# Every second low part of the summed mixing weights from ScalarE and an adding transfer instead of VectorE

## The chip, the core and the metric

The kernel runs on one core of a Trainium2 chip. The metric is the device time of one execution in microseconds (us); lower is better. A core has five engines that work side by side and each take their instructions in a fixed order: TensorE (PE in the profile; PEld is its loading of stationary operands), VectorE (DVE), ScalarE (ACT), GpSimd (POOL) and SyncE (SP, which here only starts transfers). Transfers are started from SP, ACT and POOL and are carried out by 16 shared DMA engines.

## The reference

The layer has an attention branch and a gated branch over the same normalised input; the change is in the gated branch (`B`).

```python
def _B_ref(x, w_in, w_sp, b_sp, w_out):
    z = _gelu(jnp.einsum("bsd,df->bsf", x, w_in))
    z1 = z[..., :Fh]
    z2 = _layernorm(z[..., Fh:], axis=-1)
    g = jnp.einsum("ts,bsf->btf", w_sp, z2) + b_sp[None, :, None]
    return jnp.einsum("bsf,fd->bsd", z1 * g, w_out)

xn = _layernorm(x, axis=-1)
s = _A_ref(xn, A_wqkv, A_wo)       # 32 heads, 8 taps at distance 2
g = _silu(_B_ref(xn, B_w_in, B_w_sp, B_b_sp, B_w_out))
return x + s * g
```

There are 2048 rows (`S`), 512 features (`D`) and 896 hidden features (`Fh`). `w_sp` is the 2048 x 2048 mixing matrix. All inputs are float32.

## The kernel before

**Two parts for each operand.** TensorE multiplies in a rounded 32-bit form (`F32R`). To keep float32 accuracy, each operand is held as a high part (the value rounded) and a low part (what the rounding left), and each product is three matmuls: high by high, high by low, low by high. `split` (L194) makes the parts: ScalarE copies the raw block into the high tile, which rounds it, and VectorE then writes raw minus high into the low tile. `prep` (L175) fetches a raw block of 128 x 512 (256 KB) by a transfer from SP, takes the next of eight pairs of weight tiles (`whi0..7`, `wlo0..7`; a pair is free again when TensorE has used it for the last time) and calls `split`. The raw blocks go round in four buffers (tag `raw`, `RAW = 4`); one is free again when both of its readers are done.

**The stages.** In order: products for q, k and v (`qkv`, to about 100 us of the profile), the hidden products (`z1`, `z2`, to about 325 us), the mixing product (the `g` matmuls of L823, 325 to 570 us), the output of the gated branch (`b`, L1065 to L1067, to about 650 us) and that of the attention (`s`, the same lines, to the end).

**The mixing product.** It is done for two halves `a` of the columns by a scheme of seven block products, in which some weights are plain blocks of `w_sp` (`plain`, tiles `wsp_`) and some are sums and differences of blocks (`summed`, tiles `ws_`). Those sums were written to the scratch tensor `sums_d` earlier. `block_product` takes eight weight blocks `s` in four pairs. For a pair it runs three matmuls for each of three feature blocks (`ODD`) and each of the two weights, and in some products for a fourth (`odd`). Four products use summed weights, for each half: m6, m7, m5 and m3, so there are 64 such blocks. They stand on TensorE in the order m6a, m6b, m7 (two halves), then m4 with plain weights, m5a, m5b, m3a, m3b.

**What fills the other engines.** The attention is worked on by VectorE during the whole of this time, at a low priority. Its units (`sub`, `h`) have two steps of four rows each: `scores` (tile `pr`), `heads` (tile `lg`), `weighted` (tile `pv`), and in `finish` the folds and a transpose (tile `tt`). The first fold of `pv` (L631) is on POOL, which also starts the loads of `k`, `q` and `v` and the store of `tt` to `o_d`. POOL further stores gates to `g_d` (L914).

**What sets the order.** A scheduler builds each engine's order ahead of time from priorities and its own estimates of times; `pin` keeps some instructions in the order of the program. On the chip each engine only follows its list and waits on semaphores.

Of the kernel before, what the change touches and what calls it, by code (L numbers as in the profile page):

```python
# [11 lines left out]
F32 = mybir.dt.float32  # L12
F32R = mybir.dt.float32r
AF = mybir.ActivationFunctionType
ALU = mybir.AluOpType
# [11 lines left out]
CT = 512  # L27
# [30 lines left out]
def kernel(  # L58
# [13 lines left out]
    nc = tc.nc  # L72
    pins = [True]
    lows, highs, sums_of = [], [], []

    def pin(ins):
        return tc.keep_in_program_order(ins) if pins[0] else ins
# [22 lines left out]
    sums_d = dram.tile([2, 2, HT, P, 2, CT], F32, name="sums_d")  # L100
# [59 lines left out]
    def weight_pair(name):  # L160
        i = next(slot)
        return (
            wts.tile([P, 512], F32R, tag=f"whi{i}", name=name + "h"),
            wts.tile([P, 512], F32R, tag=f"wlo{i}", name=name + "l"),
        )

    def fetch(src, n, name):
        raw = raws.tile([P, 512], F32, tag="raw", name=name + "r", bufs=RAW)
        pin(nc.sync.dma_start(raw[:, :n], src))
        return raw  # L170
# [4 lines left out]
    def prep(src, n, name, raw=None, pair_=None):  # L175
        if raw is None:
            raw = fetch(src, n, name)
        hi, lo = pair_ or weight_pair(name)
        split(hi[:, :n], lo[:, :n], raw[:, :n])
        return hi, lo  # L180

    @contextmanager
# [11 lines left out]
    def split(hi, lo, src):  # L194
        first_ = pin(nc.scalar.activation(hi, src, AF.Copy))  # L195
        highs.append(first_)
        lows.append(pin(nc.vector.tensor_tensor(lo, src, hi.bitcast(F32), op=ALU.subtract)))  # L197
        return first_
# [225 lines left out]
    def weights(g, raw=[None] * KB):  # L424
        return [prep(wqkv[:, g, k, :], GC, f"wqkv_{g}_{k}", raw=raw[k]) for k in range(KB)]
# [69 lines left out]
    for k in range(KB):  # L495
        hi, lo = [planes[:, FB - KB + k, :JC, a] for a in range(2)]
# [196 lines left out]
    for f in range(FB):  # L693
        pair_ = side_pair("w1_last") if f == FB - 1 else None
        wh, wl = prep(w_in1[:, f, :], KB * P, f"w1_{f}", pair_=pair_)
        for c in range(NC):
            pz = mm(f"z1_{f}_{c}")
            for k in range(KB):
                cc = slice(k * P, (k + 1) * P)
                xh, xl = [planes[:, FB - KB + k, c * JC : (c + 1) * JC, a] for a in range(2)]  # L700
                nc.tensor.matmul(pz, wh[:, cc], xh, start=k == 0, stop=False)
                nc.tensor.matmul(pz, wh[:, cc], xl, start=False, stop=False)
                nc.tensor.matmul(pz, wl[:, cc], xh, start=False, stop=k == KB - 1)
            if c % 2 == 0:
                zp = t4(f"z1t_{f}_{c}")
            zt = zp[:, c % 2]
            nc.scalar.activation(zt, pz, AF.Gelu_apprx_tanh)  # L707
            if c % 2:
                nc.scalar.dma_start(z1_d[f, c - 1 : c + 1].rearrange("c p t -> p c t"), zp)
        if f == 2:  # L710
            first_sums(*z1_sums[FB])
        if f < FB - 1:
            first_sums(*z1_sums[f + 1])

    HALF = (slice(0, 512), slice(512, FH))
    WID = (512, FH - 512)
    w2 = {
        (k, h): prep(w_in2[:, k, HALF[h]], WID[h], f"w2_{k}_{h}")
        for h in range(2)
        for k in range(KB)  # L720
# [115 lines left out]
    for n in range(8):  # L836
        a, f = n // 2 % 2, n // 4 * 2 + n % 2
# [30 lines left out]
        return w  # L868

    def summed(a, half_, i):  # L870
        return lambda s: prep(sums_d[a, half_, s, :, i], CT, f"ws_{a}{half_}{i}_{s}")

    def operand(i, s0):
        f0, r0 = ((ODD + 1, 0), (0, 0), (0, HT))[i]
# [122 lines left out]
    def kept(a):  # L997
# [19 lines left out]
    stored_gates(1, 2)  # L1017
    block_product(
        0, "m6a", at(0, LAST), summed(0, 0, 0),
        steps=([T4[0]], [T4[1], seeds], [T4[2]], [T4[3]]),  # L1020
    )
    spill(0)
    block_product(1, "m6b", at(0, LAST), summed(1, 0, 0))
    spill(1)
    vs3 = triple("x3")
    for a in range(2):
        block_product(
            a, "m7", at(0, 0), summed(a, 0, 1), odd(0),
            steps=([T1[2 * a]], [], [T1[2 * a + 1]], []),
        )  # L1030
        for f in range(ODD):
            evict(a, f, vs3[a][f])
# [144 lines left out]
```

## Time and profile before

| what | value |
|---|---|
| median of 3 runs | 696.28 us (693.53 to 700.32) |
| span of the profiled execution | 694.8 us |
| its own time | the page gives its span; the three runs lie between 1.3 us below and 5.5 us above it |
| TensorE, VectorE, ScalarE, POOL busy | 99%, 90%, 40%, 31% of the span |
| granted TensorE clock | 0.999 of full speed |
| summed-weight products on TensorE | 385.2 to 461.6 us (m6, m7), 504.9 to 570.4 us (m5, m3) |

A row of a timeline gives the start (us), the duration (us), the engine, the line, the operation, the output and inputs, and in brackets how long the engine had been idle before and what ended it. A row that groups instructions gives their number, the busy time, the mean in ns, and the idle time before them with what released it. In the rows of stretches stand, after the stretch and its length, the busy times of PE, PEld, DVE, ACT and POOL with the numbers of instructions, the granted clock, the mean share of the DMA engines and GB/s.

### The profile page before, as it was taken

To read this page: it belongs to the slowest core of one execution; us is meant where nothing else is said; L and a number is where in the kernel's file an instruction comes from. 1 tells how busy PE (TensorE), PEld (TensorE's weight loads), DVE (VectorE), ACT (ScalarE), POOL (GpSimd) and SP (SyncE) were. 2 spreads that over 40 slices of the span, in tenths; PEclk is the share of its full clock that TensorE was granted. 3 is DMA by queue.
4 is the path that set the end of the run, shared out by engine and by line. 5 is a ranking of instruction groups with operands and counts; after the bars stand their busy time and mean duration, and the time that the engine had idled before them with its cause. 6 is when DMAs were issued, how large, how long until landed. Compare 5 with 4: busy or idle time off the path is not lost.

```text
span 694.8 us, 9233 instructions
## 1 busy us (share of the span) xinstructions
PE 688.0 (99%) x3084; PEld 572.9 (82%) x3084; DVE 624.9 (90%) x866; ACT 276.2 (40%) x458; POOL 213.3 (31%) x242
## 2 busy tenths in 40 slices
PE   8999999999999999999999999999999999999998
PEld 7888888888888899977888888888888887888886
DVE  6777877999999989899999998999998999999875
ACT  4343333314424256765533544342433444211432
POOL 3105737282343321223123222214021111452320
PEclk9999999999999999999999999999999999999999
DMA  8869899959999865266798878667576683645797
GB/s 269 253 191 303 273 361 374 334 200 352 406 410 363 320 227 189 96 212 221 260 401 281 289 222 305 203 224 264 158 255 215 221 306 118 242 155 167 253 339 267
DMA packets 102223, 182.36 MB, mean 262 GB/s; under 512 B 9184, under 2 KB 45280, under 8 KB 102176
## 3 DMA queue, kind: packets, MB, share of 16 engines
q1 hardware_dynamic: 56624, 102.21, 43.7%
q0 software_dynamic: 13824, 52.24, 20.8%
q10 hardware_dynamic: 31728, 27.33, 11.6%
q8 instruction: 24, 0.39, 0.2%
q14 instruction: 23, 0.19, 0.1%
HBM read 122.42 MB, written 59.32 MB: 262 GB/s over the span
## 4 chain that ended last, share of the span: by engine, by line
PE 68%; DVE 15%; DMA 8%; issue 4%; ACT 3%; POOL 1%; DVEq 0%; ACTq 0%; POOLq 0%; SPq 0%
PE g L823 35%; PE qkv L385 4%; PE qkv L387 4%; PE qkv L386 4%; PE b L1066 4%; PE b L1065 4%; PE b L1067 4%; DMA sb<-in_w_sp 3%; DVE lg L580 2%; DVE pr L573 2%; PE s L1066 2%; PE s L1067 2%; PE s L1065 2%; DMA sums_d<-sb 2%; PE qkv L308 2%
## 5 line engine op out<-in xcount | busy, mean ns | idle before, releaser
L631 POOL TENSOR_TENSOR pv<-pv 128x1024 f32<-128x1024 f32 x29 | 69.6, 2400 | 97.1 <-DVE pv L620 85.1
L573 DVE TENSOR_TENSOR pr<-k,q 128x2048 f32<-128x2048 f32 x32 | 73.6, 2300 | 4.3 <-DMA k<-qkv_d 4.1
L620 DVE TENSOR_TENSOR pv<-v,lg 128x2048 f32<-128x2048 f32 x32 | 74.6, 2331 | 0.9 <-DMA v<-qkv_d 0.4
L580 DVE TENSOR_REDUCE lg<-pr 128x128 f32<-128x2048 f32 x32 | 73.0, 2280 | 0.1
L645 POOL DMA_DIRECT2D o_d<-tt x32 | 18.0, 562 | 141.4 <-DVE tt L644 140.9
L433 ACT ACTIVATE stage<-qkv 128x512 f32<-128x512 f32 x40 | 23.0, 590 | 29.7 <-DMA qkv_d<-stage 19.7
L805 POOL DMA_DIRECT2D ol<-o_d x32 | 17.7, 555 | 36.8 <-DVE BIG L197 11.0
L707 ACT ACTIVATE z1t<-z 128x512 f32<-128x512 f32 x28 | 15.5, 596 | 28.9 <-DMA z_d<-z1t 13.5
L728 PE MATMUL z<-w_0h,BIG 128*128 128x512 f32 x64 | 25.0, 391 | 0.8 <-ACT zt L731 0.8
L1076 ACT ACTIVATE bt<-b 128x512 f32<-128x512 f32 x16 | 9.3, 594 | 39.8 <-PE b L1067 39.8
L730 PE MATMUL z<-w_0h,BIG 128*128 128x512 f32 x64 | 25.0, 391 | 0.0
L729 PE MATMUL z<-w_0l,BIG 128*128 128x512 f32 x64 | 25.0, 391 | 0.0
L752 ACT ACTIVATE zt<-zt,nmz,mvz 128x896 f32<-128x896 f32 x16 | 17.5, 1131 | 18.5 <-POOL nmz L746 18.5
L740 DVE BATCH_NORM_STATS2 zst<-zt 128x6 f32<-128x448 f32 x32 | 19.3, 613 | 6.1 <-ACT zt L731 6.0
L280 DVE TENSOR_TENSOR xT<-xT,mr 128x512 f32<-128x512 f32 x20 | 13.8, 688 | 11.8 <-DMA mr<-mv_d 6.8
L636 DVE TENSOR_TENSOR pv<-pv 128x512 f32<-128x512 f32 x32 | 22.9, 716 | 0.0
L731 ACT ACTIVATE zt<-z 128x512 f32<-128x512 f32 (+1 forms) x32 | 15.9, 536 | 14.2 <-DMA sums_d<-sa 12.8
L730 PE MATMUL z<-w_1h,BIG 128*128 128x384 f32 x64 | 21.5, 336 | 0.0
L728 PE MATMUL z<-w_1h,BIG 128*128 128x384 f32 x64 | 21.5, 335 | 0.0
L729 PE MATMUL z<-w_1l,BIG 128*128 128x384 f32 x64 | 21.4, 335 | 0.0
L195 ACT ACTIVATE BIG<-zl 128x512 fp32r<-128x512 f32 x20 | 12.4, 629 | 22.4 <-DVE zl L893 20.6
L393 POOL TENSOR_TENSOR sb<-sa,sb 128x512 f32<-128x512 f32 x12 | 18.7, 1560 | 5.3 <-DMA sb<-in_w_sp 5.0
(478 smaller groups left out, 2303.6 us busy)
## 6 DMA issues: line engine op xcount, KB each, us to landing
qkv_d<-stage ACTq DMA_DIRECT2D x24, 512.0 KB
v<-qkv_d POOLq DMA_DIRECT2D x14, 704.0 KB, 5.3
k<-qkv_d POOLq DMA_DIRECT2D x13, 704.0 KB, 6.4
sums_d<-sa POOLq DMA_DIRECT2D x14, 512.0 KB, 7.5
sums_d<-sb POOLq DMA_DIRECT2D x14, 512.0 KB, 7.8
z_d<-z1t ACTq DMA_DIRECT2D x14, 512.0 KB
zl<-z_d SPq DMA_DIRECT2D x12, 512.0 KB
tr<-t_d SPq DMA_DIRECT2D x12, 384.0 KB
```

The costliest lines, as they stand in the source:

```text
L385: nc.tensor.matmul(pq, xh[:, k], wh, start=k == 0, stop=False)
L573: line(nc.vector.tensor_tensor(pr, taps(ks[u], j0), qb.unsqueeze(1).to_broadcast([P, W, NJ * CS]), op=ALU.mult))
L580: line(nc.vector.tensor_reduce(lgs[u][:, :, j0 * HS : (j0 + NJ) * HS], pr.rearrange("p w (i d) -> p w i d", d=DH), axis=AX.X, op=ALU.add,))
L620: line(nc.vector.tensor_tensor(pv.rearrange("p w (i d) -> p w i d", d=DH), taps(vs[u], j0).rearrange("p w (i d) -> p w i d", d=DH), lgs[u] ...
L631: eng.tensor_tensor(pv[:, 0:4], pv[:, 0:4], pv[:, 4:8], op=ALU.add)
L728: nc.tensor.matmul(pz, xh[:, k], wh, start=k == 0, stop=False)
L729: nc.tensor.matmul(pz, xh[:, k], wl, start=False, stop=False)
L730: nc.tensor.matmul(pz, xl[:, k], wh, start=False, stop=k == KB - 1)
L823: nc.tensor.matmul(pg, z[a], w[b], start=start and i == 0, stop=stop and i == 2, skip_group_check=seeded)
L1065: nc.tensor.matmul(pp[:, cols], hi, wh, start=k == 0, stop=False)
L1066: nc.tensor.matmul(pp[:, cols], hi, wl, start=False, stop=False)
L1067: nc.tensor.matmul(pp[:, cols], lo, wh, start=False, stop=k == n - 1)
```

## The change

For blocks with an odd `s` (32 of the 64) the low part is made in another way. ScalarE writes the high part as before. ScalarE then writes minus the rounded block into the low tile, and a transfer started from POOL adds the float32 block from `sums_d` to the low tile in place. The result is again raw minus rounded. It is written as float32 by the transfer. VectorE has no part in it. The ScalarE instruction for the low tile is entered in `highs`, behind which the `seeds` are placed. Blocks with an even `s` are made as before.

```diff
+    def prep_added(src, name):
+        raw = fetch(src, CT, name)
+        hi, lo = weight_pair(name)
+        nc.scalar.activation(hi, raw, AF.Copy)
+        highs.append(nc.scalar.activation(lo, raw, AF.Copy, scale=-1.0))
+        nc.gpsimd.dma_start(lo.bitcast(F32), src, accum_op=ALU.add)
+        return hi, lo
+
     def summed(a, half_, i):
-        return lambda s: prep(sums_d[a, half_, s, :, i], CT, f"ws_{a}{half_}{i}_{s}")
+        return lambda s: (prep_added if s % 2 else lambda src, name: prep(src, CT, name))(
+            sums_d[a, half_, s, :, i], f"ws_{a}{half_}{i}_{s}"
+        )
```

The numbers of lines below the new function move by 8 (by 10 behind `summed`). The scheduler places the work anew. On POOL, at the first product with summed weights (m6a, and the start of m6b), the list before reads as follows, beginning at the store of an attention step; `pv` is the fold of a step, `g_d` the store of gates.

```order
L645 DMA o_d<-tt_4_1542 128x256
L631 TENSOR_TENSOR pv_0_1551<-pv_0_1551 128x1024
L914 DMA g_d<-zl_0_3829 128x2x512
L914 DMA g_d<-zl_2_3836 128x2x512
L645 DMA o_d<-tt_0_1571 128x256
L631 TENSOR_TENSOR pv_4_1574<-pv_4_1574 128x1024
L562 DMA v_0_1586<-qkv_d 128x1408
```

With the change the list at the same place is this; the transfers of L187 are the new ones.

```order
L653 DMA o_d<-tt_4_1542 128x256
L187 DMA ws_3l<-sums_d 128x512
L639 TENSOR_TENSOR pv_0_1551<-pv_0_1551 128x1024
L187 DMA ws_5l<-sums_d 128x512
L924 DMA g_d<-zl_0_3829 128x2x512
L924 DMA g_d<-zl_2_3836 128x2x512
L187 DMA ws_7l<-sums_d 128x512
L187 DMA ws_1l<-sums_d 128x512
L653 DMA o_d<-tt_0_1571 128x256
L187 DMA ws_3l<-sums_d 128x512
L639 TENSOR_TENSOR pv_4_1574<-pv_4_1574 128x1024
L570 DMA v_0_1586<-qkv_d 128x1408
```

The new transfers stand between the attention's instructions: that for `ws_3` of m6a behind a store of `tt`, that for `ws_5` behind a fold, and the next row after these is that for `ws_5` of m6b, behind a fold and the load of `v`. That for `ws_1` of m6a stands earlier, behind the load `v_1_1545`.

On VectorE, at the same place, the list before was this (`zl` are gates times banks, `BIG<-tr` low parts of combined `z2` blocks, `sm` and `lg` steps of the softmax).

```order
L197 TENSOR_TENSOR ws_2l<-ws_2r,ws_2h 128x512
L644 STREAM_TRANSPOSE tt_4_1542<-pv_4_1533 128x256
L612 TENSOR_REDUCE sm_1547<-lg_1485 128x32
L197 TENSOR_TENSOR ws_3l<-ws_3r,ws_3h 128x512
L613 RECIPROCAL sm_1547<-sm_1547 128x32
L893 TENSOR_TENSOR zl_0_3829<-g_0_3191,zl_0_3829 128x512
L614 TENSOR_TENSOR lg_1485<-lg_1485,sm_1547 128x256
L197 TENSOR_TENSOR BIG<-tr_2_3907,BIG 128x2x3x128
L197 TENSOR_TENSOR ws_4l<-ws_4r,ws_4h 128x512
L620 TENSOR_TENSOR pv_0_1551<-v_1_1545,lg_1485 128x2048
L580 TENSOR_REDUCE lg_1525<-pr_4_1538 128x8x16
```

Now it is this.

```order
L205 TENSOR_TENSOR ws_2l<-ws_2r,ws_2h 128x512
L652 STREAM_TRANSPOSE tt_4_1542<-pv_4_1533 128x256
L620 TENSOR_REDUCE sm_1547<-lg_1485 128x32
L621 RECIPROCAL sm_1547<-sm_1547 128x32
L622 TENSOR_TENSOR lg_1485<-lg_1485,sm_1547 128x256
L628 TENSOR_TENSOR pv_0_1551<-v_1_1545,lg_1485 128x2048
L588 TENSOR_REDUCE lg_1525<-pr_4_1538 128x8x16
L903 TENSOR_TENSOR zl_0_3829<-g_0_3191,zl_0_3829 128x512
L205 TENSOR_TENSOR BIG<-tr_2_3909,BIG 128x2x3x128
L205 TENSOR_TENSOR ws_4l<-ws_4r,ws_4h 128x512
L903 TENSOR_TENSOR zl_0_3829<-g_1_3192,zl_0_3829 128x512
```

`ws_3l` is gone, and the attention's `pv` now stands ahead of one gate, one low part of `tr` and `ws_4l`.

At the end of the mixing product, where the weights `wout` begin, VectorE's list before was

```order
L197 TENSOR_TENSOR ws_7l<-ws_7r,ws_7h 128x512
L893 TENSOR_TENSOR zl_4_5159<-yl_0_5161,zl_4_5159 128x512
L197 TENSOR_TENSOR wout_0l<-wout_0r,wout_0h 128x512
L893 TENSOR_TENSOR zl_6_5171<-yl_2_5173,zl_6_5171 128x512
L644 STREAM_TRANSPOSE tt_4_1745<-pv_4_1736 128x256
```

and is now

```order
L205 TENSOR_TENSOR ws_6l<-ws_6r,ws_6h 128x512
L581 TENSOR_TENSOR pr_4_1781<-k_0_1764,q_0_1765 128x2048
L205 TENSOR_TENSOR wout_0l<-wout_0r,wout_0h 128x512
L903 TENSOR_TENSOR zl_4_5187<-yl_0_5189,zl_4_5187 128x512
L644 TENSOR_TENSOR pv_4_1776<-pv_4_1776 128x512
```

The fold that follows `wout_0l` there is of the step `pv_4_1776`, two steps of the attention behind that of `pv_4_1736`: at that place VectorE has been given two steps more of attention.

## The prediction

> **What bounds the kernel now.** I read the page's busy shares first, then the busy time by stretches, then what TensorE waited for, and last the timelines of the engines around one product. From the page:
>
> ```profile
> span 694.8 us, 9233 instructions
> PE 688.0 (99%) x3084; PEld 572.9 (82%) x3084; DVE 624.9 (90%) x866; ACT 276.2 (40%) x458; POOL 213.3 (31%) x242
> ```
>
> TensorE is busy for 688.0 of 694.8 us. VectorE, which the change relieves, has 90%. The two stretches in which summed weights are made and used look like this:
>
> ```profile
> 376.00:456.00 80.00, 80.00 (x355) 66.24 (x354) 75.94 (x102) 34.97 (x58) 18.14 (x19) 1.00 0.78 265
> 490.00:570.00 80.00, 80.00 (x355) 66.24 (x354) 77.22 (x111) 30.07 (x52) 12.61 (x13) 1.00 0.69 230
> ```
>
> In both, TensorE runs 355 matmuls in 80 us, one each 0.225 us, with no gap. VectorE is almost full too (75.94 and 77.22), but what it is late with is not what TensorE waits for. All that TensorE waited for is six waits, of which the page of waits gives for the mixing product only the last three below:
>
> ```profile
> PE z L728 <- ACT zt L731: 0.8, 1, 0.8
> ...
> PE g L823 <- ACT g L841: 0.4, 1, 0.4
> PE g L823 <- DVE wsp_1l L197: 0.3, 1, 0.3
> PE g L823 <- ACT BIG L195: 0.2, 1, 0.2
> ```
>
> So TensorE's stream is the bound from end to end, and 0.9 us at most could be won in the mixing product. The rest of VectorE's work can only cost time, by being late, never save any.
>
> **The change part by part: what leaves and what comes.**
>
> ```profile
> L197 DVE TENSOR_TENSOR ws_1l<-ws_1r,ws_1h 128x512 fp32r<-128x512 f32 x8 | 5.4, 678 | 0.0
> L195 ACT ACTIVATE ws_1h<-ws_1r 128x512 fp32r<-128x512 f32 x8 | 5.1, 632 | 5.0 <-DMA ws_1r<-sums_d 4.9
> ```
>
> VectorE loses 32 subtractions of 0.678 us, 21.7 us. By its new list it gets back two steps of attention in the same time, so it stays full. ScalarE gains 32 copies of the form of `ws_1h`, 32 x 0.632 = 20.2 us, some 10 us in each stretch, where it was busy 34.97 and 30.07 of 80: covered by its own idle time. Neither is on TensorE's path, so I count 0 for both. If ScalarE's cover were gone, each low part would come 0.63 us later, and that term is in the sum below anyway, since the copy stands ahead of the transfer.
>
> POOL gains 32 starts of transfers. The DMA engines gain 32 x 256 KB = 8.4 MB in about 160 us, 52 GB/s beside 265 and 230, and the destination is read as well. They are busy 0.78 and 0.69, so there is room, but transfers will take somewhat longer.
>
> What can cost is the new chain of an odd low part: fetched raw block, high copy, low copy, POOL's turn, transfer. Before, it was raw block, high copy, VectorE's turn, 0.68 us.
>
> **The price of the adding transfer.** No transfer of this kind is in the trace. The nearest rows are transfers on POOL's queue in these stretches (KB, us from issue to landing), and plain fetches of the same 256 KB, read as the time from SP's issue to the ScalarE copy that waits for it:
>
> ```profile
> g_d<-zl POOLq DMA_DIRECT2D x3, 512.0 KB, 5.2
> o_d<-tt POOLq DMA_DIRECT2D x12, 128.0 KB, 5.1
> q<-qkv_d POOLq DMA_DIRECT2D x6, 256.0 KB, 6.5
> ```
>
> ```profile
> 380.50 0.32 SPq L169 DMA_DIRECT2D ws_5r<-sums_d  x1
> 394.11 0.32 SPq L169 DMA_DIRECT2D ws_1r<-sums_d  x1
> ```
>
> ```profile
> 387.37 0.64 ACT L195 ACTIVATE ws_5h<-ws_5r 128x512 fp32r<-128x512 f32 x1 [0.64 <-DMA ws_5r<-sums_d]
> 398.18 0.64 ACT L195 ACTIVATE ws_1h<-ws_1r 128x512 fp32r<-128x512 f32 x1 [2.36 <-DMA ws_1r<-sums_d]
> ```
>
> The fetches took 6.9 and 4.1 us. The lower end of the price is 4.1 (as fast as the faster plain fetch). The upper end is 13, twice `q`, if reading the destination and adding doubles a transfer. I take 6.5, the row of `q`: the same size on the same queue, behind another transfer as most of the new ones will be.
>
> A page would have it otherwise: the Trainium skill, "DMA: Bandwidth & Descriptors", in "Anatomy of one DMA — SWDGE (gpsimd) path", fits a transfer from this queue as 2.0 us plus its bytes over 436 GB/s, an estimate of 2.6 us here; the rows above do not bear it out in this loaded kernel (5.1 us for 128 KB), and by it the sum below would be 0.
>
> **The first product, transfer by transfer.** POOL's timeline before at m6a and the start of m6b:
>
> ```profile
> 384.47 0.55 POOL L645 DMA_DIRECT2D o_d<-tt  x1 [3.72 <-DVE tt L644]
> 390.25 2.40 POOL L631 TENSOR_TENSOR pv<-pv 128x1024 f32<-128x1024 f32 x1 [5.22 <-DVE pv L620]
> 395.14 0.73 POOL L914 DMA_DIRECT2D g_d<-zl  x1 [1.09 <-DVE zl L893]
> 407.38 0.58 POOL L645 DMA_DIRECT2D o_d<-tt  x1 [11.51 <-DVE tt L644]
> 413.45 0.57 POOL L562 DMA_DIRECT2D v<-qkv_d  x1
> ```
>
> POOL mostly waits for VectorE's attention, up to 11.51 us at one instruction, and the new transfers now stand in line behind those waits. VectorE's timeline there:
>
> ```profile
> 384.61 0.68 DVE L197 TENSOR_TENSOR ws_3l<-ws_3r,ws_3h 128x512 fp32r<-128x512 f32 x1
> 385.20 0.35 DVE L613 RECIPROCAL sm<-sm 128x32 f32<-128x32 f32 x1
> 385.45 0.64 DVE L893 TENSOR_TENSOR zl<-g,zl 128x512 f32<-128x512 f32 x1
> 386.00 0.42 DVE L614 TENSOR_TENSOR lg<-lg,sm 128x256 f32<-128x256 f32 x1
> 386.33 0.96 DVE L197 TENSOR_TENSOR BIG<-tr,BIG 128x768 fp32r<-128x768 f32 x1
> 387.19 0.70 DVE L197 TENSOR_TENSOR ws_4l<-ws_4r,ws_4h 128x512 fp32r<-128x512 f32 x1
> 387.80 2.30 DVE L620 TENSOR_TENSOR pv<-v,lg 128x2048 f32<-128x2048 f32 x1
> ```
>
> From start to start, `ws_3l` takes 0.59, the gate 0.55, `BIG<-tr` 0.86, `ws_4l` 0.61. All four no longer stand ahead of `pv`, which so starts 2.6 us earlier, at 385.2, and the fold on POOL at 387.65 (it follows by 2.45). TensorE's first uses of the low parts are the deadlines:
>
> ```profile
> 386.13 0.39 PE L823 MATMUL g<-ws_1l,BIG 128*128 128x512 f32 x1
> 390.21 0.39 PE L823 MATMUL g<-ws_3l,BIG 128*128 128x512 f32 x1
> 394.75 0.39 PE L823 MATMUL g<-ws_5l,BIG 128*128 128x512 f32 x1
> 398.37 0.39 PE L823 MATMUL g<-ws_7l,BIG 128*128 128x512 f32 x1
> 406.53 0.39 PE L823 MATMUL g<-ws_3l,BIG 128*128 128x512 f32 x1
> 410.61 0.39 PE L823 MATMUL g<-ws_5l,BIG 128*128 128x512 f32 x1
> ```
>
> With 6.5 us from start to landing, and each delay moving all later deadlines:
>
> - `ws_1` of m6a follows its two copies and starts near 379; it lands at 385.5, in time.
> - `ws_3` stands behind the store of `tt` (384.47 + 0.55), starts at 385.0, lands at 391.5: 1.3 late.
> - `ws_5` stands behind the fold (387.65 + 2.40), starts at 390.05, lands at 396.55 against 394.75 + 1.3: 0.5 late, 1.8 in all.
> - `ws_7` stands behind both stores of gates. VectorE's four gates end about 0.4 us earlier than before, so the second store runs from 394.0 to 394.75 and the transfer lands at 401.25 against 398.37 + 1.8: 1.1 late, 2.9 in all.
> - In m6b, `ws_3` follows the store of the next step. With VectorE's new order I count that store at 402.45 rather than 407.38 (five subtractions and two late gates fewer ahead of it); start 403.0, landing 409.5 against 406.53 + 2.9: 0.1 late. `ws_5` follows a fold and the load of `v`: start 407.2, landing 413.7 against 410.61 + 3.0: 0.1 late. In all 3.1.
>
> Whatever the price, the sum here is about the price less 3.4. Once TensorE has been late by that, the later products find their transfers ahead of it: m7 uses each pair for longer (a fourth feature block).
>
> **The later products.** The tightest is the last weight of m3b:
>
> ```profile
> 557.09 0.68 DVE L197 TENSOR_TENSOR ws_2l<-ws_2r,ws_2h 128x512 fp32r<-128x512 f32 x1
> 558.39 0.42 SPq L169 DMA_DIRECT2D ws_7r<-sums_d  x1
> 564.02 0.64 ACT L195 ACTIVATE ws_7h<-ws_7r 128x512 fp32r<-128x512 f32 x1
> 567.01 0.39 PE L823 MATMUL g<-ws_7l,BIG 128*128 128x512 f32 x1
> ```
>
> Its fetch goes out in SP's order once VectorE has read raw `ws_2`. Copies from 564.02 end at 565.3; a transfer then lands at 571.8 against 567.01 + 3.1: 1.7 late if VectorE comes to `ws_2l` as late as before, 0 if it comes 2 us earlier, as its list (16 subtractions out, one step of attention in up to m5) may let it. I take 0.9.
>
> Sum: 0 + 0 + 3.1 + 0.9 = 4.0 us on a span of 694.8, 698.8. The profile gives no time of its own beyond the span; the median of the three runs is 696.28, 1.5 above the span, so I forecast 700.3 as a median.
>
> **The rivals.**
>
> *The transfers are hidden.* With 4.1 us all six are in time but the last of m6a (0.5) and one of m6b (0.1); m3b is met. That gives 0.6, 696.9. For it: the faster fetch. Against it: every row of POOL's queue is above 5. The rule of the Trainium skill's page "DMA: Bandwidth & Descriptors" named above would give this case, at 696.3.
>
> *The adding transfer is slow and TensorE is fed at its pace (slower).* With 13 us the first product costs 13 - 3.4 = 9.6. A pair of tiles is used for 4.1 us in a period of 16.3 (m6a's `ws_3l` to m6b's is 406.53 - 390.21 = 16.3), which leaves 12.2 us from its release to its next use. Two copies, a start and 13 us are 14.8: 2.6 late in each of m5b, m3a and m3b, 7.8 more. Sum 17.4, 713.7. It decides by over 1% (7 us) from a price of 10.4 us. For it: the destination is read too, the DMA engines are at 0.78, and POOL's line adds waits. Against it: 512 KB on that queue took 5.2.
>
> *VectorE's relief shortens the kernel.* It would have to take away waits of TensorE, and there are 0.9 us of them in this product: 695.4 at best. That the change only shifts VectorE's work is certain from its new list.
>
> **How the numbers follow.** Chances: my forecast of a small loss (697 to 703) 0.48, hidden 0.20, slow transfer 0.29, relief 0.03. About 1% (7 us) is what a measurement of this kernel can tell from no change. The first two lie within 1%, the third above it; of the relief I leave 0.02 to a gain over 1% by something I don't see, 0.01 within. So faster 0.02, same 0.69, slower 0.29. The range goes from 695 (hidden, with the scatter of the runs) to 712, which leaves out the worse half of the slow case.
>
> **What would show it.** In the new profile TensorE should wait, in the mixing product, for transfers that write `ws_3l`, `ws_5l`, `ws_7l`, most of it between 390 and 415 us, 3 to 4 us in all; the new transfers' time from issue to landing should be 5 to 8 us; ScalarE should be busier by 20 us and VectorE less by at most that. Step by step wrong: waits in every product, near its end, would speak for the slow transfer; no waits and landings near 4 us for the hidden one; POOL idle behind attention with a weight's copies long done would mean that the line on POOL costs more than I count. I am wrong altogether if TensorE waits outside the mixing product, above all at the end, where the attention's last steps feed it.

## The result and the profile after

The changed kernel takes 713.02 us (median of 4 runs, 710.81 to 715.28), the kernel before, in the same comparison, 697.96 us (693.53 to 700.32). The ratio is 1.0232, with a 95% interval of 1.0203 to 1.0261: slower, by 15.1 us between the medians. The forecast was 700.3 us, with a range of 695 to 712. In the later comparisons the median of the kernel before lies between 695.68 and 696.91 us, so a difference of 1 to 2 us between runs of different comparisons says little.

The changed kernel's page opens with the span and the busy time of each engine:

```profile
span 710.6 us, 9277 instructions
PE 691.4 (97%) x3084; PEld 573.6 (81%) x3084; DVE 611.9 (86%) x834; ACT 291.3 (41%) x490; POOL 242.7 (34%) x274
```

The work moved as said: ScalarE has 32 instructions and 15.1 us more, VectorE 32 instructions and 13.0 us less, POOL 32 instructions and 29.4 us more. TensorE now stands idle for 19 us instead of 7. Where it does, the view by stretches tells. Its columns are busy us (instructions) of PE, PEld, DVE, ACT and POOL, then the granted TensorE clock, the busy share of the transfer engines, and GB/s:

```profile
376.00:456.00 80.00, 75.96 (x325) 61.77 (x324) 70.65 (x88) 39.52 (x69) 34.86 (x36) 0.98 1.00 301
456.00:490.00 34.00, 34.00 (x151) 28.17 (x150) 33.19 (x42) 12.44 (x22) 7.52 (x7) 1.00 0.73 243
490.00:570.00 80.00, 74.64 (x325) 60.53 (x324) 72.70 (x99) 34.75 (x62) 27.27 (x28) 1.00 0.91 260
570.00:590.00 20.00, 18.15 (x77) 14.13 (x77) 17.95 (x20) 8.22 (x15) 6.30 (x7) 1.00 0.87 273
590.00:650.00 60.00, 60.00 (x266) 49.65 (x265) 59.11 (x78) 19.61 (x35) 21.66 (x29) 1.00 0.51 171
```

In each of the two stretches with summed weights TensorE ran 325 matmuls where it ran 355, that is 30 x 0.225 = 6.8 us of work less, and the transfer engines went from 0.78 and 0.69 to 1.00 and 0.91. In between, with plain weights, and from 590 to 650 us TensorE has no gap. The table of what TensorE waited for names the blocks:

```profile
PE g L831 <- DMA ws_5l<-sums_d: 3.7, 3, 2.7
PE g L831 <- DMA ws_3l<-sums_d: 3.1, 3, 1.4
PE g L831 <- DMA ws_1l<-sums_d: 2.7, 1, 2.7
PE g L831 <- ACT g L849: 1.9, 1, 1.9
...
PE b L1075 <- ACT wout_4h L203: 1.3, 1, 1.3
```

The columns are the total, the count and the longest in us. The first three rows are adding transfers, 9.5 us, with 2.7 us at one instruction twice; a row of 0.2 us for `ws_7l` belongs to them too. These eight waits are all the waits of TensorE in the products with summed weights: it waits there for no part of an even block. The fourth row lies at 317 us, ahead of the first adding transfer (379.5 us): TensorE waits 1.9 us for a bank (`g`) that ScalarE fills, and 0.4 us in the kernel before. Why isn't known. (The mixing product is already running there: the last `z` matmul of the kernel before starts at 295 us.) The last row, for `wout_4h`, lies behind the mixing product. The view of transfers from POOL in the mixing product (KB, median us from issue to landing) gives their price, and that of their neighbours on the queue:

```profile
k<-qkv_d POOLq DMA_DIRECT2D x7, 704.0 KB, 8.2
ws_1l<-sums_d POOLq DMA_DIRECT2D x8, 256.0 KB, 7.2
ws_3l<-sums_d POOLq DMA_DIRECT2D x8, 256.0 KB, 6.9
ws_5l<-sums_d POOLq DMA_DIRECT2D x8, 256.0 KB, 6.3
ws_7l<-sums_d POOLq DMA_DIRECT2D x8, 256.0 KB, 6.2
q<-qkv_d POOLq DMA_DIRECT2D x7, 256.0 KB, 8.5
```

An adding transfer lands after 6.2 to 7.2 us; the forecast took 6.5. But `q` went from 6.5 to 8.5, and it is not part of the change. The plain fetches of the blocks suffer too, as two of them in m3a show, each from SP's issue to the ScalarE copy that waited for it:

```profile
535.49 0.32 SPq L169 DMA_DIRECT2D ws_1r<-sums_d  x1
540.08 0.32 SPq L169 DMA_DIRECT2D ws_3r<-sums_d  x1
...
540.98 0.64 ACT L186 ACTIVATE ws_1l<-ws_1r 128x512 fp32r<-128x512 f32 x1 [1.75 <-DMA ws_1r<-sums_d]
547.77 0.63 ACT L185 ACTIVATE ws_3h<-ws_3r 128x512 fp32r<-128x512 f32 x1 [3.55 <-DMA ws_3r<-sums_d]
```

They took 5.5 and 7.7 us. Over all fetches for which ScalarE waited, the mean went from 5.1 us (15 of them) to 7.7 (15) between 376 and 456 us, and from 4.4 (14) to 7.3 (7) between 490 and 590 us. So the blocks come 2.6 to 2.9 us later, the even ones among them, in whose making nothing was changed. The means are over the fetches that ScalarE had to wait for, not over all. No term of the forecast's sum had this.

### The profile page after: what moved, and what is told of

Same layout as the page of the kernel before. It is cut to its first block, busy times and chain, and to the rows that moved or that the text cites. A ratio compares the mean times of both kernels' runs of the same rounds, so it can differ in the third digit from the quotient of the medians.

```text
span 710.6 us, 9277 instructions
## 1 busy us (share of the span) xinstructions
PE 691.4 (97%) x3084; PEld 573.6 (81%) x3084; DVE 611.9 (86%) x834; ACT 291.3 (41%) x490; POOL 242.7 (34%) x274
## 4 chain that ended last, share of the span: by engine, by line
PE 30%; DVE 30%; DMA 25%; issue 8%; ACT 4%; POOL 1%; SPq 0%; DVEq 0%; ACTq 0%; POOLq 0%
PE g L831 11%; DVE lg L588 4%; DMA sb<-in_w_sp 4%; PE b L1076 3%; PE b L1077 3%; PE b L1075 3%; DVE pr L581 3%; DMA qkv_d<-stage 3%; DVE pv L628 2%; DMA ws_2r<-sums_d 2%; PE s L1076 2%; PE s L1077 2%; PE s L1075 2%; DVE BIG L205 2%; PE qkv L316 2%
## 5 line engine op out<-in xcount | busy, mean ns | idle before, releaser
L715 ACT ACTIVATE z1t<-z 128x512 f32<-128x512 f32 x28 | 15.5, 596 | 28.6 <-DMA z_d<-z1t 17.7
L1136 DVE TENSOR_TENSOR sg<-s,sg 128x512 f32<-128x512 f32 (+2 forms) x17 | 11.1, 658 | 15.1 <-PE s L1077 14.9
L752 POOL TENSOR_TENSOR mvz<-mvz,nhalf 128x2 f32<-128x2 f32 x8 | 8.6, 1071 | 41.8 <-DVE mvz L751 41.8
L739 ACT ACTIVATE zt<-z 128x512 f32<-128x512 f32 (+1 forms) x32 | 15.8, 536 | 13.7 <-DMA sums_d<-sa 11.4
```

## The experiments

Two explanations stood against each other, with a third beside them:

- *Chain*: TensorE loses by waiting for the odd low part itself, whose way now has a second copy, POOL's turn and a landing in it.
- *Load*: the added transfers fill the shared transfer engines, all fetches come later, and TensorE loses whether or not it waits for an adding transfer.
- *Line*: POOL's longer line holds back attention's first folds, and through them VectorE and the buffers.

"The kernel before" is run beside each experiment, and each difference is taken to that. A sum that is left out is named; otherwise the kernel computes the reference.

**No transfer.** The odd low part is only ScalarE's copy; the block is not added to it.

```diff
-        nc.gpsimd.dma_start(lo.bitcast(F32), src, accum_op=ALU.add)
```

> As the changed kernel, without the 32 adding transfers: an odd low part is only the ScalarE copy, so the block itself is left out of it. It keeps the 32 ScalarE copies and VectorE's relief. If the loss of 15 us comes from the transfers (their way to TensorE, their traffic, or their place in POOL's line), this takes 694 to 700 us. If ScalarE's extra 20 us or VectorE's new list cost anything by themselves, it takes 703 us or more.

699.02 us against 696.91, ratio 1.0023 (0.9997 to 1.0050). The 32 copies and VectorE's new list are worth some 2 us (by the interval, 0 to 3.5). In the profile TensorE has no gap in the summed products; it waits 2.9 us for `wout_4h` behind them. The rest of the loss comes with the transfers.

**A plain transfer.** It overwrites the low part, so the subtraction is left out. The lists of TensorE, ScalarE, POOL and SyncE are those of the changed kernel; on VectorE two instructions are exchanged.

```diff
-        nc.gpsimd.dma_start(lo.bitcast(F32), src, accum_op=ALU.add)
+        nc.gpsimd.dma_start(lo.bitcast(F32), src)
```

> As the changed kernel, but the 32 transfers overwrite the low part and don't add to it, so the subtraction is left out. Same bytes out of memory, same queue, same chain, same order of TensorE's matmuls. If reading the destination and adding makes the transfer dear, the landings fall from 6.2 to 7.2 us to below 5 and the kernel takes 705 us or less. If the place in the chain and in POOL's line is what costs, it takes 710 to 714 us with landings above 5.5.

704.36 us against 696.91, ratio 1.0091 (1.0060 to 1.0122): half of the loss. The landings are 5.1 to 5.8 us, 1 to 1.5 us shorter. Since the lists are the same, the other half of the loss comes from what adding changes in the transfer, and not from an order. The page's table of queues (packets, MB, share of 16 engines' span) of the kernel before, the changed one and this one has the rest:

```profile
q0 software_dynamic: 13824, 52.24, 20.8%
```

```profile
q0 software_dynamic: 18432, 60.63, 26.8%
```

```profile
q0 software_dynamic: 16384, 60.63, 23.6%
```

A share times 16 engines times the span is engine time. Before, it is 0.208 x 16 x 694.8 = 2312 us. The changed kernel has 735 us more, 23.0 per transfer, in 144 packets each; this kernel (span 702.6) has 341 more, 10.6 per transfer, in 80 packets. For the same bytes an adding transfer occupies the transfer engines about twice as long as a plain one.

**The transfers beside the product.** VectorE makes all low parts; the transfers add into a scratch in memory.

```diff
-        raw = fetch(src, CT, name)
-        hi, lo = weight_pair(name)
-        nc.scalar.activation(hi, raw, AF.Copy)
-        highs.append(nc.scalar.activation(lo, raw, AF.Copy, scale=-1.0))
-        nc.gpsimd.dma_start(lo.bitcast(F32), src, accum_op=ALU.add)
...
+        hi, lo = prep(src, CT, name)
+        nc.gpsimd.dma_start(next(spares), src, accum_op=ALU.add)
```

> VectorE makes all low parts as before; in addition POOL starts the same 32 adding transfers of the same blocks, into a scratch in memory that nobody reads. The traffic and POOL's line are as in the changed kernel, TensorE waits for none of them. If traffic or the folds that are pushed late by POOL's longer line were the main cause, it takes 708 us or more. If TensorE loses by waiting for the transfers themselves, it takes 696 to 702 us.

720.24 us against 696.91. It tells nothing of the question: nothing held the transfers back, and POOL started them between 184.7 and 327.5 us, ahead of the products with summed weights. A later run holds them in their places.

**The halves.** The change in m6 and m7 alone, then in m5 and m3 alone.

```diff
-        return lambda s: (prep_added if s % 2 else ...
+        return lambda s: (prep_added if s % 2 and half_ == 0 else ...
```

> The change in the first two summed products (m6, m7) alone, 16 transfers; m5 and m3 as before. In the changed kernel TensorE had lost 6.6 us by the end of m7. If the losses of the two halves add, this takes 703 to 706 us. If the later products depend on the first having been late (their transfers then find more room), it takes as much and the second half alone will take more than 9 us over the kernel before.

> The change in the last two summed products (m5, m3) alone, 16 transfers. The first half alone cost 4.9 us. If the halves add up to the 15 to 16 us of the whole, this takes 706 to 709 us, with TensorE waiting for low parts in m3. If the loss in m5 and m3 needs the late start from the first half, it takes 702 us or less; if the late start had helped, 711 us or more.

The first takes 701.83 us, ratio 1.0076 (1.0047 to 1.0104), 4.9 us more; the second (`half_ == 1`) 705.32 us, ratio 1.0131 (1.0099 to 1.0162), 8.7 us more. Together they are 13.6 of the 15.1 us: about additive, and the later half is the dearer one. The fetches are late only where the transfers are: 7.9 and 5.0 us in the first run, 4.8 and 7.1 in the second.

**Half the transfers, spread out.** The weights 1 and 5 of each eight.

```diff
-        return lambda s: (prep_added if s % 2 else ...
+        return lambda s: (prep_added if s % 4 == 1 else ...
```

> All four products, but only the weights 1 and 5 of each eight are made with the adding transfer: 16 transfers, one in 20 us of TensorE's stream where the changed kernel has two. If the loss grows evenly with the transfers, it takes 704 to 706 us. If it comes from transfers that queue behind each other and behind attention on POOL and fill the transfer engines, half of them cost much less than half: 697 to 702 us, with landings of 5 to 6 us.

709.82 us, ratio 1.0180 (1.0132 to 1.0228), with runs from 704.94 to 712.63. Neither expectation held: 16 transfers cost about as much as 32. So the loss is not in proportion to the number of the transfers; what it does follow this run doesn't show.

**Beside the product, in their places.** VectorE makes all low parts; each transfer waits for VectorE's low part and adds into a scratch in memory of its own.

```diff
...
+        hi, lo = prep(src, CT, name)
+        ins = nc.gpsimd.dma_start(spares[len(used)], src, accum_op=ALU.add)
+        tc.add_manual_dep(ins.ins, lows[-1].ins.name, SYNC, reason="behind the low part")
+        used.append(ins)
```

> VectorE makes all low parts as before. POOL starts the same 32 adding transfers at nearly the same places of its line, each behind the low part by VectorE, into a scratch in memory that nobody reads. TensorE waits for none of them. If the traffic and the folds pushed late by POOL's line cost by themselves, it takes 703 us or more and TensorE waits for VectorE's or ScalarE's parts. If TensorE loses only by waiting for the transfers' own landings, it takes 695 to 701 us.

715.16 us, ratio 1.0263 (1.0232 to 1.0293). TensorE waits for none of the transfers and loses 18.6 us, no less than with the change (713.02 us would be 16.4 us above the kernel before of this comparison). What it waits for now, by its table:

```profile
PE g L833 <- DVE ws_5l L207: 4.3, 1, 4.3
PE g L833 <- DVE ws_1l L207: 3.3, 2, 1.9
PE b L1077 <- ACT wout_3h L205: 2.5, 1, 2.5
```

The first two rows are parts that VectorE makes from blocks that came late (the fetches took 6.9 and 6.6 us in the mean); the third lies behind the product. The chain is not needed for a loss.

**Folds on VectorE.** All first folds of attention on VectorE, in the changed kernel and, as a control, in the kernel before.

```diff
-            first_fold(part, nc.gpsimd if coming else nc.vector)
+            first_fold(part, nc.vector)
```

> The changed kernel with all of attention's first folds on VectorE and none on POOL: POOL's line holds transfers alone in these stretches, and no fold can run beside VectorE's sums of two operands. If the folds ahead of the transfers on POOL and their contention with VectorE make the late half of the loss, it takes 703 to 708 us. If the landing itself is what is late, 711 us or more. VectorE gets some 1 us more for each fold, and a loss by that would show as VectorE's work at the end of the kernel.

> Control for the run with the folds on VectorE (721.63 us): the kernel before with all first folds on VectorE. If the folds on POOL make part of the loss of the change, this takes 707 us or more (VectorE is nearly full, so the folds cost there), and the change adds less than its 15 us to it. If they have no part in it, it takes about 706 us or less, and the change adds 15 us or more.

The changed kernel takes 721.63 us this way (ratio 1.0358, 1.0317 to 1.0399), the kernel before 723.48 (1.0389, 1.0360 to 1.0418). In the control TensorE has no gap in the mixing product and waits for attention at the end:

```profile
PE s L1065 <- ACT o_3h L195: 6.8, 2, 5.9
PE s L1065 <- ACT BIG L195: 4.5, 1, 4.5
```

The changed kernel still loses some 10 us in the product (75.27 and 76.91 busy of 80 us, then 18.07 of 20), without a fold on POOL, but has no such waits at the end. So the product loses without folds on POOL too. That the times come out even would fit VectorE's relief paying at the end, where the control waits; no run tests that.

**Load from another queue.** VectorE makes all low parts and POOL is left alone; ScalarE's queue copies 512 KB from memory to memory behind each odd high part. Then the same with 256 KB.

```diff
...
+        hi, lo = prep(src, CT, name)
+        ins = nc.scalar.dma_start(spares[len(used)][:, :, :CT], both)
+        tc.add_manual_dep(ins.ins, highs[-1].ins.name, NOSYNC, reason="behind the high part")
+        used.append(ins)
```

> VectorE makes all low parts as before, and POOL is left as before. ScalarE's queue copies 512 KB from memory to memory (a plain transfer of 256 rows, nobody reads it) behind each odd high part: traffic for the transfer engines without POOL's line and without a wait of TensorE for it. If the load of the transfer engines alone makes the weights' blocks late (they took 7.3 to 7.7 us in the changed kernel, 4.4 to 5.1 before), this takes 703 us or more with fetches above 6.5 us. If POOL's line is what costs, it takes 695 to 700 us.

> Traffic alone from ScalarE's queue, 256 KB a time instead of 512 KB: the bytes of the changed kernel's transfers, plain. The plain transfers on POOL's queue that TensorE waits for gave 704.36 us. If that loss is the traffic's, this takes 702 to 707 us. If the loss starts only where the transfer engines are full (share 0.97 with 512 KB), it takes 696 to 700 us.

With 512 KB it takes 715.17 us (ratio 1.0277, 1.0235 to 1.0319), with 256 KB 700.19 (1.0059, 1.0034 to 1.0084). The queue of ScalarE in the kernel before, with 512 KB, and with 256 KB:

```profile
q10 hardware_dynamic: 31728, 27.33, 11.6%
```

```profile
q10 hardware_dynamic: 40432, 44.11, 18.3%
```

```profile
q10 hardware_dynamic: 36336, 35.72, 15.4%
```

By the sum used above, a 512 KB copy takes 24.6 us of engine time (span 709.8) and a 256 KB copy 13.5 (span 699.1): the first is the load of an adding transfer, the second a little over that of a plain one. 24.6 us a time cost 19.5 us here; 23.0 cost 15.1 in the changed kernel and 18.6 beside the product. 13.5 cost 3.9, the longest wait being one of 2.1 us for `o_3h` at 685 us, far behind the product; 10.6, with TensorE waiting for them, 7.5. In these runs the loss grows much faster than the load: with 256 KB the transfer engines stand at 0.91 in the first stretch and TensorE has no gap there, with 512 KB they stand at 0.97 and it has 2.2 us:

```profile
376.00:456.00 80.00, 80.00 (x354) 66.25 (x353) 75.95 (x101) 36.39 (x59) 18.15 (x19) 1.00 0.91 316
```

```profile
376.00:456.00 80.00, 77.82 (x336) 63.63 (x335) 73.79 (x97) 30.91 (x52) 18.13 (x20) 0.98 0.97 340
```

The Trainium skill says in "DMA: Bandwidth & Descriptors", section "Issuing engines are not separate DMA queues", that transfers run on the same 16 engines whichever engine starts them. The runs agree: SP's fetches come later whether POOL starts the load (6.9 and 6.6 us) or ScalarE (512 KB: 6.8 and 6.2 us).

**The line without the load.** As beside the product, but 8 rows (16 KB) a time.

```diff
-        ins = nc.gpsimd.dma_start(spares[len(used)], src, accum_op=ALU.add)
+        ins = nc.gpsimd.dma_start(spares[len(used)][:8], src[:8], accum_op=ALU.add)
```

> As the run with the low parts by VectorE and the transfers into a scratch beside them (715.16 us), but each transfer moves 8 rows, 16 KB, instead of 256 KB. POOL's places and waits stay, the traffic goes. If traffic is the cause, it takes 695 to 701 us. If POOL's line (transfers that wait for weights, attention's folds behind them) is the cause, it takes 708 us or more.

696.03 us, ratio 1.0002 (0.9992 to 1.0012). 32 starts on POOL, each of which waits for a weight ahead of attention's folds, cost nothing (POOL is busy 31.57 of 80 us here, 18.14 before). The line is out as a cause by itself. The 18.6 us come with the bytes. With them the lists have changed too: 175 of VectorE's 866 places differ from the kernel before in the run with 256 KB, 7 in this one. So a part of the 18.6 us can be the order's; no run separates the two.

**The chain without the load.** As the changed kernel, with 8 rows of 128 added; the block is left out of the other rows.

```diff
-        nc.gpsimd.dma_start(lo.bitcast(F32), src, accum_op=ALU.add)
+        nc.gpsimd.dma_start(lo[:8].bitcast(F32), src[:8], accum_op=ALU.add)
```

> As the changed kernel, but each adding transfer adds 8 rows of 128 (16 KB); for the other rows the block is left out of the low part. The chain for TensorE stays: copy, copy, POOL's turn, a start, a landing. The traffic goes. If the load of the transfer engines makes most of the loss, by late fetches and by its own landing, it takes 698 to 703 us. If the place behind attention in POOL's line makes it, it takes 707 us or more.

706.13 us, ratio 1.0157 (1.0107 to 1.0207): 10.5 us, between the two expectations. The transfer engines stand at 0.77 and 0.72, the fetches at 5.3 and 4.5 us, as before, and TensorE waits all the same. So the chain alone is enough for a loss too (the lists are near those of the changed kernel, not the same: 117 of VectorE's 834 places differ). Its longest wait, followed back through the timelines of VectorE, SP, ScalarE, POOL and TensorE:

```profile
531.77 1.99 DVE L205 TENSOR_TENSOR ws_4l<-ws_4r,ws_4h 128x512 fp32r<-128x512 f32 x1
...
533.78 0.32 SPq L169 DMA_DIRECT2D ws_1r<-sums_d  x1
...
539.22 0.63 ACT L186 ACTIVATE ws_1l<-ws_1r 128x512 fp32r<-128x512 f32 x1 [4.17 <-DMA ws_1r<-sums_d]
...
540.16 0.84 POOL L187 DMA_DIRECT2D ws_1l<-sums_d  x1 [1.44 <-ACT ws_1l L186]
...
546.00 0.50 PE L831 MATMUL g<-ws_1l,BIG 128*128 128x512 f32 x1 [2.28 <-DMA ws_1l<-sums_d]
```

VectorE, whose subtraction took 1.99 us instead of 0.68, frees a raw buffer at 533.76; the fetch goes out at once and takes 5.4 us, the copies 0.9, the transfer 5.8 for its 16 KB. POOL is idle and waits for ScalarE, not the other way round. From the freed buffer to TensorE it is 12.2 us, where before it would have been the 5.4, a copy and one subtraction.

**Load without the chain.** As the changed kernel with ScalarE's copies, but the transfers add into scratches in memory; the block is left out of the odd low parts.

```diff
-        nc.gpsimd.dma_start(lo.bitcast(F32), src, accum_op=ALU.add)
...
+        ins = nc.gpsimd.dma_start(spares[len(used)], src, accum_op=ALU.add)
+        tc.add_manual_dep(ins.ins, highs[-1].ins.name, SYNC, reason="behind the low part")
+        used.append(ins)
```

> As the changed kernel with ScalarE's copies and VectorE's relief, but the adding transfers of 256 KB go into a scratch in memory that nobody reads, each behind the copy that makes the low part; the block itself is left out of it. TensorE waits for ScalarE's copy alone. If the loss is TensorE's own wait for the landings, it takes 696 to 702 us. If it is traffic and the line on POOL, it takes 706 us or more.

716.63 us, ratio 1.0301 (1.0277 to 1.0325). TensorE needs only ScalarE's copy of an odd low part, and now waits for the even ones, by VectorE: 4.2 us for one `ws_6l`, 1.9 for a `ws_4l`. Fetches took 7.7 and 7.0 us.

**Six raw buffers.** `RAW = 6` and, for the room, `WIDE = 7`: the kernel before, the changed kernel, and the 512 KB load from ScalarE's queue.

```diff
-RAW = 4
-WIDE = 8
+RAW = 6
+WIDE = 7
```

> Control: the kernel before, with six raw buffers instead of four and seven wide tiles instead of eight (their room). If the ring of four does not hold the kernel before (TensorE waited 0.9 us in the product), it takes 693 to 700 us; if the wide tiles that are taken away cost, more.

> The changed kernel with six raw buffers and seven wide tiles. If the later fetches (7.3 to 7.7 us instead of 4.4 to 5.1) cost because only four raw buffers go round, most of the loss goes: 698 to 704 us, beside the control's time. If the low parts' own transfers and POOL's line are late, it takes 709 us or more.

> Traffic alone (the run with 512 KB copies on ScalarE's queue, 715.17 us) with six raw buffers and seven wide tiles. If the ring of four turns the slower fetch into a lower rate of blocks, it takes 697 to 705 us. If single late transfers or other loads than the weights' hold TensorE, 710 us or more.

The control takes 741.82 us: the two sizes together cost 45 us, ahead of the product and at the end (one wait of 13.9 us of the `g` matmuls that fill the banks for the second half, 15.1 us for `o_3h`). So total times are no measure here; the control's product itself has no gap. The load of 512 KB costs 3.2 us in this form (745.06), instead of 19.5. The same load from the same queue, by stretches, with six buffers:

```profile
376.00:456.00 80.00, 77.15 (x341) 63.56 (x340) 79.83 (x106) 32.80 (x56) 20.99 (x20) 1.00 1.02 371
...
490.00:570.00 80.00, 80.00 (x355) 66.24 (x354) 79.48 (x114) 32.35 (x54) 15.03 (x14) 1.00 0.89 311
570.00:590.00 20.00, 20.00 (x90) 16.57 (x89) 18.24 (x27) 8.08 (x14) 2.10 (x4) 1.00 1.01 374
```

The transfer engines are as full as with four. From 490 us on TensorE has no gap, and in the first stretch it waits once, 2.9 us for a bank that ScalarE fills (`g`), and for no weight; with four buffers it had waited for weights in both. That fits a ring: eight blocks go through TensorE in 16.3 us (from the prediction's rows), so each of four raw buffers has to come round in 8.2 us, and 7.7 us of fetch (the mean of the changed kernel) with a copy and a subtraction behind it don't fit into that.

In the changed kernel six buffers (732.98 us) cure less. It has no gap from 376 to 456 us either, at a share of 1.01, but it loses 7.2 us from 490 to 570 and 2.3 from there to 590, where it waits for adding transfers (2.1, 1.7, 2.0 and 2.3 us) and once for attention (1.4). Its products with summed weights lose 14.1 us in all, as much as with four buffers (table below). So the ring of four is not what the whole loss hangs on. The work lies some 15 us later in these kernels than in those with four buffers, so this stands a little less firm than the runs at equal places.

**Where the leads were long.** In the kernel before, the time from the end of an odd high copy to TensorE's first use of the low part is 6.0 to 15.5 us in m7 and m5a and 2.4 to 9.7 in the others. The change in m7 and m5a alone, 12 transfers:

```diff
-        return lambda s: (prep_added if s % 2 else ...
+        return lambda s: (prep_added if s % 2 and (a, half_, i) in ((0, 0, 1), (1, 0, 1), (0, 1, 1)) else ...
```

> The change only in m7 (both halves) and m5a, 12 transfers. There the kernel before has 6.0 to 15.5 us from the end of an odd high copy to TensorE's first use of the low part (median 10.5), in m6, m5b and m3 2.4 to 8.6 us. If a part is late where its lead is shorter than copy, POOL's turn and landing (about 8 us), these 12 cost 0 to 2 us: 695 to 698.5 us. If every transfer costs about the same by its traffic (15 us over 32), they cost 5 to 6 us: 701 to 703 us.

710.31 us, ratio 1.0212 (1.0182 to 1.0242): 13.7 us for 12 transfers, against both expectations. The longest wait is in m5a, where the lead of `ws_3` had been 13.0 us:

```profile
501.78 0.32 SPq L169 DMA_DIRECT2D ws_3r<-sums_d  x1
...
508.83 0.63 ACT L203 ACTIVATE BIG<-ul 128x512 fp32r<-128x512 f32 x1 [4.68 <-DMA ul<-g_d]
...
509.89 0.62 ACT L186 ACTIVATE ws_3l<-ws_3r 128x512 fp32r<-128x512 f32 x1
...
510.94 0.87 POOL L187 DMA_DIRECT2D ws_3l<-sums_d  x1 [2.08 <-ACT ws_3l L186]
...
518.24 0.50 PE L831 MATMUL g<-ws_3l,BIG 128*128 128x512 f32 x1 [3.74 <-DMA ws_3l<-sums_d]
```

The copies of `ws_3` stand in ScalarE's line behind a copy that waits 4.68 us for another load, and the transfer takes 7.3. The fetch went out 12.7 us ahead of the moment at which TensorE was ready for the block (518.24 - 3.74). A lead read from the kernel before is therefore no promise: each version has new lists, and its raw buffers come free at other times. Why this list is so much worse than that of the 16 transfers of m6 and m7 (4.9 us) isn't settled.

**By products.** From the start of the first matmul with summed weights to that of the last, in us, from TensorE's timelines of the runs above:

| run | m6 and m7 | m5 and m3 |
|---|---|---|
| the kernel before | 75.93 | 65.05 |
| the changed kernel | 82.53 | 72.34 |
| the chain without the load | 77.91 | 72.34 |
| beside the product, in their places | 79.54 | 74.57 |
| load without the chain | 76.85 | 78.79 |
| six raw buffers, the kernel before | 75.93 | 65.05 |
| six raw buffers, the changed kernel | 75.93 | 79.19 |

The chain alone gives 2.0 of the 6.6 us that the changed kernel loses in m6 and m7, and the same 7.3 us in m5 and m3. Load alone gives a loss too, at other places: 0.9 and 3.6 us in the first two products, 9.5 and 13.7 in the last two.

## Why the prediction was wrong, point by point

- *TensorE's stream is the bound, nothing is to be won.* Right.
- *What leaves and what comes, 0.* Nearly right: without the transfers 2.1 us, with an interval that takes in none. The profile has them at a wait for `wout_4h` behind the product (2.9 us there, 1.3 in the changed kernel). The forecast had named waits outside the product as the sign that it is wrong altogether; they are a small part of the loss.
- *"They are busy 0.78 and 0.69, so there is room, but transfers will take somewhat longer."* This is the step that failed first. The room was not there: the shares went to 1.00 and 0.91, because an adding transfer takes 23 us of engine time and not the 10.6 of a plain one, and the fetches that ScalarE waited for went from 4.4 to 5.1 us to 7.3 to 7.7. The sum had no term for that. Load without the chain costs 18.6 to 21.0 us (transfers that nobody waits for), and 0.3 us when the bytes go.
- *The price of the adding transfer, 6.5 us.* Right as a median (6.2 to 7.2), and wrong where TensorE waited in m6 and m7: those three transfers took 8.8, 9.8 and 9.1 us. The second was started at 407.99 and ended TensorE's wait at 417.85 us (that row stands in the last section):

```profile
407.99 0.92 POOL L187 DMA_DIRECT2D ws_5l<-sums_d  x1
```

They were 0.66, 2.67 and 0.72 us late, so with 6.5 us from the same starts all three would have been in time. That is an estimate from the rows; it says that in these products the loss came by way of long landings, in a stretch where the transfer engines stand at 1.00. The five transfers that TensorE waited for in m5 and m3 took 6.0, 5.1, 8.2, 6.7 and 5.5 us: most of these were late before they started. The Trainium skill's figure for a transfer from this queue ("DMA: Bandwidth & Descriptors", section "Anatomy of one DMA — SWDGE (gpsimd) path", as in the prediction) gave an estimate of 2.6 us; the measurement doesn't bear it out. Nor would the sum have been 0 by it: by the prediction's own rows the last part of m3b would land at 567.9 against 567.01, up to 0.9 us late.
- *The first product, 3.1 us, and m7, 0.* Measured are 6.6 us in these products, and 4.9 us with the change in them alone. The mechanism was seen, the places were not: `ws_3` of m6a was 0.66 late (1.3 forecast), `ws_5` and `ws_7` of m6a were in time (0.5 and 1.1 forecast), `ws_5` of m6b was 2.67 late (0.1 forecast), `ws_5` of m7 0.72 (0 forecast). The two of m6a were in time because the change moves work on TensorE too: the odd low matmuls of a pair now stand behind those of all feature blocks, so `ws_7l` of m6a, first used at 398.37 before, comes at 404.37 us in TensorE's timeline (below). The forecast had read the new lists of VectorE and POOL and not TensorE's.

```profile
404.37 0.39 PE L831 MATMUL g<-ws_7l,BIG 128*128 128x512 f32 x1
```

- *The later products, 0.9 us.* The second step that failed. They cost 8.7 us with the change in them alone, and 7.3 us in the changed kernel. One transfer had been taken for the tightest and the rest for covered by the late start of the first product. In fact a block's way there begins with the raw buffer that comes free; with a second copy, a start and a landing behind the fetch it took 12.2 us at the longest wait of the chain without the load, and that chain loses 10.5 us, 7.3 of them here.
- *POOL's line.* It took most of the working and had little part: at the eight waits of the changed kernel the transfer was started 1.0 to 3.1 us after the two copies began (the copies take some 1.2), and the line without the bytes costs 0.3 us.
- *The rivals.* The slow adding transfer gave 713.7 us, close to what came, but that is chance: it needed a price of 13 us, and the loss of the first product would have been 9.6 us. The hidden transfers' 0.6 us don't follow from the prediction's own rows: with 4.1 us the last part of m3b would land at 569.4 against 567.01 + 0.6, 1.8 us late if VectorE comes as late as before, so that case should have had the same 0.9 us there.

Load and chain don't add up: 18.6 to 21.0 and 10.5 us apart, 15.1 together. A wait for the one may give the other time; that isn't tested. In the changed kernel the rows speak for the load, by way of the landings, in m6 and m7, where the chain alone gives 2.0 of 6.6 us; and for the chain in m5 and m3, where it gives as much alone as with the load. But load alone loses in m5 and m3 too, the lists differ from run to run, and each row is from one profile, so how the 15.1 us divide stays open.

## What to carry to other kernels

A transfer costs twice: its landing for the one who waits for it, and its engine time for all others. Where transfer engines stand near 0.8, price the second first: engine time per transfer, from the table of queues, times the number, against the room that is left. And where blocks go through a small ring of buffers, compare the ring's period (buffers times the time per block) with fetch and use. Here a deeper ring took away the waits for weights under load alone, and not the loss of the changed kernel. And read the new list of the engine that is the bound, not only the lists of its helpers.

## What had not been expected of the hardware

An adding transfer of 16 KB landed after 3.4 to 5.1 us and one of 256 KB after 6.2 to 7.4; a plain one of 256 KB after 5.1 to 5.8 (medians; the transfer engines stand at 0.72 to 0.78 with 16 KB, at 0.82 to 1.00 with 256 KB). So most of a landing doesn't come from the size here.

The clock fell after one wait and not after another of the same length. In the changed kernel, TensorE waits 2.67 us in m6b, and its matmuls then go from a start each 0.23 us to one each 0.43, from 418.94 to 421.93: 7 matmuls, 1.4 us beyond the wait itself. Three of them:

```profile
417.85 0.50 PE L831 MATMUL g<-ws_5l,BIG 128*128 128x512 f32 x1 [2.67 <-DMA ws_5l<-sums_d]
...
419.37 0.63 PE L831 MATMUL g<-ws_5h,BIG 128*128 128x512 f32 x1
419.80 0.63 PE L831 MATMUL g<-ws_6h,BIG 128*128 128x512 f32 x1
```

The granted clock by stretches (the column behind POOL's) shows it there, and shows full speed after the wait of 2.72 us that ended at 550.28:

```profile
420.00:422.00 2.00, 2.00 (x7) 1.54 (x6) 1.90 (x4) 1.01 (x2) 0.57 (x1) 0.50 1.00 400
...
552.00:554.00 2.00, 2.00 (x10) 1.69 (x9) 2.00 (x2) 1.58 (x3) 0.14 (x1) 1.00 1.00 290
```

The Trainium skill's page "TensorE: Matmul & The Clock Gate", section "Why this matters for your kernels", asks for no idle gaps above some 3 us; here 2.67 us was enough once and 2.72 was not the other time.

One contention was seen, but not tried by itself: where a fold on POOL ran beside a subtraction of two operands on VectorE in the changed kernel, the subtraction took 2.32 us instead of 0.68, and the raw buffer came free as much later.

```profile
532.21 2.69 POOL L639 TENSOR_TENSOR pv<-pv 128x1024 f32<-128x1024 f32 x1
...
533.14 2.32 DVE L205 TENSOR_TENSOR ws_4l<-ws_4r,ws_4h 128x512 fp32r<-128x512 f32 x1
```
